# Holding six V blocks in SBUF, wider outer products and an earlier zero fill in a decode-step backward kernel

## The chip, the cores and the metric

The kernel runs on one core of a Trainium2 chip. The metric is the device time of one execution in microseconds (us), as the median of several executions. Every run quoted here is of the state that the records call fast. Ratios are the record's: fast runs of one kernel over fast runs of the other, so they are not quite the ratios of the medians that are quoted beside them.

The profile names the core's engines PE (matmuls; PEld loads their weights), DVE (vector operations), ACT (scalar operations), POOL (GpSimd) and SP (SyncE, which here only issues transfers). SBUF is the core's on-chip memory. Transfers run on 16 DMA engines.

## The reference

One decode step of a transformer layer with its backward pass: two batch rows, one query position, 32 query heads on 8 key/value heads, a cache of 32,768 positions of which the last W = 4,096 are attended, and a gated feed-forward network. It returns the output and the gradients of all inputs. Cut to what matters:

```python
W = min(4096, max(256, Sk // 4))
k = jnp.repeat(k_cache[:, :, Sk - W:, :], rep, axis=1)
v = jnp.repeat(v_cache[:, :, Sk - W:, :], rep, axis=1)
p = _softmax(jnp.einsum("bhqd,bhkd->bhqk", q, k) * Dh ** -0.5, axis=-1)
o = jnp.einsum("bhqk,bhkd->bhqd", p, v)
...
_out, _vjp = jax.vjp(_f, A_x, A_k_cache, A_v_cache, A_wq, A_wo, B_w_gate, B_w_up, B_w_down)
return (out, *_vjp(grad_out))
```

The gradients of the two caches have the caches' full shape, 2 x 8 x 32768 x 128 in bf16. Only the last 4,096 positions are not zero. So seven eighths of two 134 MB tensors must be written as zeros, 235 MB. That is the largest piece of work in the kernel.

## The kernel before

There are 16 blocks (2 batch rows x 8 key/value heads) of 4,096 x 128 values, 1 MB each. K and V are each read twice: once in the forward pass, and once in the backward pass, because they don't all fit in SBUF. Loads and results go through one queue (issued by SyncE, "the load queue"), the zeros through another (issued by GpSimd).

```python
# the zero fill: 32 jobs of 7 MB from one zero tile of 128 x 4096 (8 KB a partition)
zt = const.tile([P, Z], BF16, name="zero")
nc.vector.memset(zt[:], 0.0)
...
zf.dma_start(out=dst[:, a0:a1, :], in_=src)

# forward: oT = V^T P; a V block's buffer is free as soon as it has been used
for blk in range(NBLK):
    vb = b8.tile([P, KT, DH], BF16, tag="b8", name="vb")       # b8: 17 buffers of 8 KB a partition
    ld.dma_start(out=vb[:], in_=A_v_cache[b, g, R0:SK, :]...)
    for kt in range(KT):
        nc.tensor.matmul(out=oT_ps[...], lhsT=vb[:, kt, :], rhs=PTk[...], ...)
# ... output projection, feed-forward, its backward pass and weight gradients ...

# dV (and later dK): outer products, 32 rows x 128 columns at a time, 512 matmuls for each
def dkv_block(blk, S2, blk2, o_ap, nm):
    stg = b8.tile([P, KT, DH], BF16, tag="b8", name="stg_" + nm)
    for kt0 in range(0, KT, 2 * KG):
        for r in range(2):
            ...
            for i, kt in enumerate(kts):
                nc.tensor.matmul(out=ps[:, i, :], lhsT=S2[pb:pb + HQ, kt // 2, :], rhs=blk2[pb:pb + HQ, g, :], ...)
            evac(stg[:, kts[0]:kts[-1] + 1:2, :], ps[:, 0:n, :], "f32")
    ld.dma_start(out=o_ap[b, g, R0:SK, :]..., in_=stg[:])

# backward: all 16 V blocks are loaded again
for bank in range(NBANK):
    for bl in range(BPB):
        vb = b8.tile([P, KT, DH], BF16, tag="b8", name="vb2")
        ld.dma_start(out=vb[:], in_=A_v_cache[b, g, R0:SK, :]...)
        ...
```

## Time and profile before

| | before |
|---|---|
| median of 16 runs | 878.82 us (878.42 to 882.61) |
| span of the profiled run | 876.7 us |
| busy: PE, DVE, ACT | 48%, 32%, 23% |
| bytes moved | 364.13 MB, of which 234.88 MB zeros |
| mean rate | 415 GB/s |

From the page of the kernel before: the DMA rows of the table that cuts the span into 40 equal slices (busy tenths of the 16 DMA engines, and what they moved), then three lines of the queue table (packets, MB, share of the 16 engines' time). Queue q0 is the zero fill, q1 the load queue, q8 brings the PE's instructions.

```profile
DMA  8999999999999999999999999999999999999995
GB/s 343 426 425 425 426 426 426 426 427 425 426 426 426 425 423 420 417 414 418 419 419 419 404 425 425 426 425 426 423 425 422 419 423 420 428 420 422 420 421 214
...
q0 software_dynamic: 29184, 234.88, 64.0%
q1 hardware_dynamic: 18960, 128.47, 35.2%
q8 instruction: 42, 0.69, 0.3%
```

The transfer engines are full in 38 of 40 slices. No compute engine is at half. So a change gains only if it takes bytes away, raises the rate, or shortens the start or the tail.

The load queue's own waits of the kernel before, two lines of them (the waiting queue and line, what it waited for, us in total, times, longest):

```profile
SPq L560 <- DVE stg_dk L117: 151.1, 16, 24.8
SPq L688 <- DMA out_dram<-zero: 84.8, 1, 84.8
```

The first wait sits inside the chain of loads and results: a result waits for its eviction. It looks costly. The second says why it isn't: after its last result the load queue still waits 84.8 us for zeros. The chain may get longer by about that much before it sets the time.

The tail of the kernel before, in steps of 2 us (columns: window, its length, then busy us and instruction count of PE, PEld, DVE, ACT and POOL, the granted clock, the share of the DMA engines, GB/s):

```profile
862.00:864.00 2.00, 0.00 (x0) 0.00 (x0) 0.00 (x0) 0.00 (x0) 0.00 (x0) 0.50 0.89 373
864.00:866.00 2.00, 0.00 (x0) 0.00 (x0) 0.00 (x0) 0.00 (x0) 0.00 (x0) 0.50 0.44 184
866.00:868.00 2.00, 0.00 (x0) 0.00 (x0) 0.00 (x0) 0.00 (x0) 0.00 (x0) 0.50 0.26 111
868.00:870.00 2.00, 0.00 (x0) 0.00 (x0) 0.00 (x0) 0.00 (x0) 0.00 (x0) 0.50 0.16 70
870.00:872.00 2.00, 0.00 (x0) 0.00 (x0) 0.00 (x0) 0.00 (x0) 0.00 (x0) 0.50 0.13 53
872.00:874.00 2.00, 0.00 (x0) 0.00 (x0) 0.00 (x0) 0.00 (x0) 0.00 (x0) 0.50 0.06 25
```

Within 12 us the DMA share falls from 0.89 to 0.06: the 16 engines don't finish together. The last one alone holds the kernel open.

The issue of the first zero job in the kernel before (start, duration, engine, line, operation):

```profile
1.45 1.76 DVE L149 MEMSET zero<- 128x2048 uint32 x1 [0.38 <-issue]
...
3.53 1.00 POOL L185 DMA_DIRECT2D out_dram<-zero  x1 [1.72 <-DVE x_f L274]
```

And two lines of the costliest groups, the outer products (busy us, mean ns of one, idle time before them):

```profile
L557 PE MATMUL ps_dv<-DOblk,P_bf 32*128 32x128 bf16 x512 | 56.1, 295 | 0.2
...
L557 PE MATMUL ps_dk<-Qblk,dS_bf 32*128 32x128 bf16 x512 | 49.8, 299 | 8.3 <-DVE stg_dk L117 5.6
```

### The profile page before, as it was taken

The page shows a single profiled execution, that of the slowest core. Times are in us where ns is not written, and L with a number is a line of the kernel's source. Part 1 is how long each engine was busy: PE and PEld are TensorE (multiplying, and loading weights), DVE is VectorE, ACT ScalarE, POOL GpSimd, SP SyncE. Part 2 cuts the span into 40 slices and gives each one's busy share as a digit, 9 for nine tenths or more (in the row PEclk, how much of TensorE's full clock was granted, in tenths as well). Part 3 has the DMA queues.
Part 4 walks back from the last instruction along what each step waited for, and adds up shares of the span by engine and source line. Part 5 has one row for each costly group of instructions (what it writes and reads, how often), then busy time and mean ns, then how long its engine had stood idle before and what let it go on. Part 6 is the DMA issues. An engine that isn't in the chain of part 4 may idle for free.

```text
span 876.7 us, 12218 instructions
## 1 busy us (share of the span) xinstructions
PE 423.9 (48%) x5419; PEld 306.5 (35%) x5419; DVE 282.2 (32%) x428; ACT 197.4 (23%) x297; POOL 31.7 (4%) x49
## 2 busy tenths in 40 slices
PE   0777714236187664999400476784333332870000
PEld 0776604132154521376300466663222222420000
DVE  2233260011035679777300143353222221370000
ACT  0233320000023312666300132342211121240000
POOL 4000000000000000000000000000000000000000
PEclk9958755557579855555555587865555555865555
DMA  8999999999999999999999999999999999999995
GB/s 343 426 425 425 426 426 426 426 427 425 426 426 426 425 423 420 417 414 418 419 419 419 404 425 425 426 425 426 423 425 422 419 423 420 428 420 422 420 421 214
DMA packets 48197, 364.13 MB, mean 415 GB/s; under 512 B 2568, under 2 KB 2576, under 8 KB 4880
## 3 DMA queue, kind: packets, MB, share of 16 engines
q0 software_dynamic: 29184, 234.88, 64.0%
q1 hardware_dynamic: 18960, 128.47, 35.2%
q8 instruction: 42, 0.69, 0.3%
q14 instruction: 11, 0.09, 0.0%
HBM read 81.01 MB, written 282.33 MB: 414 GB/s over the span
## 4 chain that ended last, share of the span: by engine, by line
DMA 57%; PE 23%; DVE 6%; ACT 2%; issue 1%; SPq 1%; ACTq 0%; DVEq 0%
DMA kb<-in_A_k_cache_dram 26%; DMA vb<-in_A_v_cache_dram 21%; PE ps_dv L557 6%; DMA wd<-in_B_w_down_dram 5%; DMA out_dram<-stg_dv 5%; DVE dO_row L231 2%; PE tpb L242 2%; PE ps_wo L594 2%; PE ps_dk L557 2%; PE ps_wq L660 1%; PE dxn_ps L646 1%; PE dqT_ps L632 1%; PE tpw L643 1%; PE dxn_ps L506 1%; PE tpw L519 1%
## 5 line engine op out<-in xcount | busy, mean ns | idle before, releaser
L242 PE MATMUL tpb<-ident_bf,vb 128*128 128x128 bf16 x512 | 45.4, 266 | 82.3 <-DMA vb<-in_A_v_cache_dram 81.3
L117 DVE CAST stg_dk<-ps_dk 128x512 bf16<-128x512 f32 x64 | 42.4, 688 | 111.1 <-PE ps_dk L557 106.7
L242 PEld LDWEIGHTS <-vb 128*128 128x128 bf16 x512 | 41.8, 124 | 84.7 <-DMA vb<-in_A_v_cache_dram 82.9
L117 DVE COPY vt_sb<-tpb 128x1024 bf16<-128x1024 bf16 x39 | 26.4, 690 | 113.9 <-PE tpb L242 113.2
L115 ACT CAST stg_dk<-ps_dk 128x512 bf16<-128x512 f32 x64 | 36.6, 586 | 116.7 <-PE ps_dk L557 115.1
L632 PE MATMUL dqT_ps<-dSTk,kb 128*128 128x4 bf16 x512 | 16.3, 167 | 93.8 <-DMA kb<-in_A_k_cache_dram 93.8
L557 PE MATMUL ps_dv<-DOblk,P_bf 32*128 32x128 bf16 x512 | 56.1, 295 | 0.2
L242 PE MATMUL tpb<-ident_bf,kb 128*128 128x128 bf16 x512 | 48.2, 277 | 16.5 <-DMA kb<-in_A_k_cache_dram 16.1
L557 PE MATMUL ps_dk<-Qblk,dS_bf 32*128 32x128 bf16 x512 | 49.8, 299 | 8.3 <-DVE stg_dk L117 5.6
L185 POOL DMA_DIRECT2D out_dram<-zero x32 | 28.9, 986 | 678.4 <-DMA out_dram<-zero 676.7
L115 ACT COPY vt_sb<-tpb 128x1024 bf16<-128x1024 bf16 x25 | 25.1, 1013 | 122.0 <-PE tpb L242 110.5
L242 PEld LDWEIGHTS <-kb 128*128 128x128 bf16 x512 | 44.2, 129 | 18.5 <-DMA kb<-in_A_k_cache_dram 17.6
L632 PEld LDWEIGHTS <-kb 128*128 128x128 bf16 x512 | 15.0, 105 | 97.6 <-DMA kb<-in_A_k_cache_dram 97.2
L117 DVE CAST stg_dv<-ps_dv 128x512 bf16<-128x512 f32 x64 | 44.3, 691 | 12.0 <-PE ps_dv L557 9.5
L557 PEld LDWEIGHTS <-P_bf 32*128 32x128 bf16 x512 | 39.5, 122 | 17.4 <-issue 11.3
L117 DVE COPY kt_sb<-tpb 128x1024 bf16<-128x1024 bf16 x39 | 26.5, 690 | 57.2 <-PE tpb L242 52.3
L115 ACT CAST stg_dv<-ps_dv 128x512 bf16<-128x512 f32 x64 | 37.4, 585 | 18.9 <-PE ps_dv L557 18.9
L557 PEld LDWEIGHTS <-dS_bf 32*128 32x128 bf16 x512 | 31.5, 127 | 22.5 <-issue 21.2
L115 ACT COPY kt_sb<-tpb 128x1024 bf16<-128x1024 bf16 x25 | 25.2, 1012 | 54.4 <-PE tpb L242 45.5
L361 PE MATMUL oT_ps<-PTk,vb 128*128 128x4 bf16 x512 | 15.4, 167 | 42.0 <-DMA vb<-in_A_v_cache_dram 42.0
L361 PEld LDWEIGHTS <-vb 128*128 128x128 bf16 x512 | 14.6, 104 | 42.8 <-DMA vb<-in_A_v_cache_dram 42.8
L320 PE MATMUL st_ps<-QT_bf,kt_sb 128*128 128x4 bf16 x512 | 18.5, 166 | 4.7 <-ACT kt_sb L115 3.4
(203 smaller groups left out, 546.2 us busy)
## 6 DMA issues: line engine op xcount, KB each, us to landing
out_dram<-zero POOLq DMA_DIRECT2D x32, 7168.0 KB, 207.6
kb<-in_A_k_cache_dram SPq DMA_DIRECT2D x32, 1024.0 KB, 23.2
vb<-in_A_v_cache_dram SPq DMA_DIRECT2D x32, 1024.0 KB, 39.5
out_dram<-stg_dv SPq DMA_DIRECT2D x16, 1024.0 KB, 41.4
out_dram<-stg_dk SPq DMA_DIRECT2D x16, 1024.0 KB, 14.1
wq<-in_A_wq_dram SPq DMA_DIRECT2D x4, 1024.0 KB, 11.0
wo<-in_A_wo_dram SPq DMA_DIRECT2D x4, 1024.0 KB, 42.6
out_dram<-stg_wo SPq DMA_DIRECT2D x4, 1024.0 KB, 27.8
```

The source lines that it names most:

```text
L115: nc.scalar.copy(out=out, in_=in_)
L117: nc.vector.tensor_copy(out=out, in_=in_)
L185: zf.dma_start(out=dst[:, a0:a1, :], in_=src)
L231: nc.vector.tensor_copy(out=o, in_=ps[0:B, 0:n, :])
L242: nc.tensor.transpose(out=tp[:, i, :], in_=src[:, j0 + i, :], identity=ident_bf[:])
L320: nc.tensor.matmul(out=st_ps[:, bl, kt, :], lhsT=kt_sb[:, kt, :], rhs=QT_bf[:, b, g * REP:(g + 1) * REP], start=True, stop=True)
L361: nc.tensor.matmul(out=oT_ps[:, blk * REP:(blk + 1) * REP], lhsT=vb[:, kt, :], rhs=PTk[:, kt, blk * REP:(blk + 1) * REP], start=(kt == 0), ...
L506: nc.tensor.matmul(out=dxn2_ps[:], lhsT=dT_bf[:, r, :], rhs=wT[:].rearrange("p c d -> p (c d)"), start=(n_mm == 0), stop=(n_mm == 2 * FR - 1))
L519: nc.tensor.transpose(out=tp[:, c, :], in_=wo_slice(r)[:, c * P:(c + 1) * P], identity=ident_bf[:])
L557: nc.tensor.matmul(out=ps[:, i, :], lhsT=S2[pb:pb + HQ, kt // 2, :], rhs=blk2[pb:pb + HQ, g, :], start=True, stop=True, tile_position=(pb, 0))
L594: nc.tensor.matmul(out=ps[:], lhsT=o_row[:, r:HD:RW], rhs=dh_bf[:], start=True, stop=True)
L632: nc.tensor.matmul(out=dqT_ps[:, blk * REP:(blk + 1) * REP], lhsT=kb[:, kt, :], rhs=dSTk[:, kt, blk * REP:(blk + 1) * REP], start=(kt == 0 ...
```

## The change

Its intent is to take traffic out of a kernel bound by traffic, and to use the matmul array better. Six of the 16 V blocks stay in SBUF from the forward pass to the backward pass. The buffers for that come from smaller pools. The outer products take four 128-column tiles in one matmul of 128 rows x 512 columns, with a masked operand that puts zeros where heads don't belong together. The first two zero jobs are issued ahead of the masks. The core of the diff:

```diff
-    NB8=17,
+    NB8=19,
+    N_HOLD=6,
+    NWT=2,
...
-    b4 = ctx.enter_context(tc.tile_pool(name="b4", bufs=2))
-    t2k = ctx.enter_context(tc.tile_pool(name="t2k", bufs=4))
-    t4k = ctx.enter_context(tc.tile_pool(name="t4k", bufs=2))
-    tT = ctx.enter_context(tc.tile_pool(name="tT", bufs=2))
-    wt = ctx.enter_context(tc.tile_pool(name="wt", bufs=3))
+    b4 = ctx.enter_context(tc.tile_pool(name="b4", bufs=3))
+    t2k = ctx.enter_context(tc.tile_pool(name="t2k", bufs=3))
+    t4k = ctx.enter_context(tc.tile_pool(name="t4k", bufs=1))
+    tT = ctx.enter_context(tc.tile_pool(name="tT", bufs=1))
+    wt = ctx.enter_context(tc.tile_pool(name="wt", bufs=CFG["NWT"]))
...
-        nc.vector.memset(zt[:], 0.0)
+        nc.vector.memset(zt[:, 0:zh], 0.0)
+        ... nc.gpsimd.memset(zt[:, zh:Z], 0.0)
+    NZ_FIRST = 2
+    for o_, i_ in zjobs[:NZ_FIRST]:          # ahead of the identity and mask tiles
+        zf.dma_start(out=o_, in_=i_)
...
+        if blk >= NBLK - NHOLD:
+            v_held[blk] = vb
...
-    def dkv_block(blk, S2, blk2, o_ap, nm):
+    def dkv_block(blk, S4, X4t, o_ap, nm):
+        R = wt.tile([P, NS, DH], BF16, tag="wt", name="R_" + nm)
+        nc.vector.tensor_tensor(out=R[:], in0=_bcast(X4t[b][:], 1, NS), in1=_bcast(mask4[:, g, :], 2, DH), op=ALU.mult)
+        for kk in range(NQ):
+            nc.tensor.matmul(out=ps[:].rearrange("p s d -> p (s d)"), lhsT=S4[:, b, kk, :],
+                             rhs=R[:].rearrange("p s d -> p (s d)"), start=True, stop=True)
+            evac(stg[:, NS * kk:NS * kk + NS, :], ps[:], "f32")
...
+            if blk in v_held:
+                vb = v_held[blk]
+            else:
+                vb = b8.tile(...); ld.dma_start(...)
```

The probabilities are also kept in another layout for this (bf16, four tiles side by side). The rows of the attention output are built again where they are needed, which frees one 8 KB buffer early.

More of the change, by code (lines that the diff above doesn't have):

```diff
@@ L22 @@
     STOP=99,
-    RELIEF=(),
     HOLD_WQ=1,
+    ZORDER=0,
+    N_HOLD=6,
+    NWT=2,
 )
@@ L82 @@
     EPS = 1e-5
-    assert DH == P and NCOL * 2 == P and KT % 2 == 0 and D % P == 0 and F % P == 0 and D <= 512
+    assert DH == P and NCOL * 2 == P and KT % 4 == 0 and D % P == 0 and F % P == 0 and D <= 512
     assert HQ == 32 and W % P == 0
@@ L117, in evac @@
             nc.vector.tensor_copy(out=out, in_=in_)
+    x_bf = sm.tile([B, D], BF16, tag="sm", name="x_bf")
+    ld.dma_start(out=x_bf[:], in_=A_x[:, 0, :])
+    go_bf = keep.tile([B, D], BF16, name="go_bf")
+    ld.dma_start(out=go_bf[:], in_=grad_out[:, 0, :])
+    zjobs = []
+    if R0 > 0:
+        assert R0 % P == 0
+        per_part = (R0 // P) * DH
+        Z = _gdiv_le(per_part, CFG["ZMAX"])
+        na = per_part // Z
+        zt = const.tile([P, Z], BF16, name="zero")
+        zh = (Z // 2) if Z % 2 == 0 else Z
+        nc.vector.memset(zt[:, 0:zh], 0.0)
+        if zh < Z:
+            nc.scalar.activation(out=zt[:, zh:Z], in_=zt[:, 0:Z - zh], func=ACTF.Copy, scale=0.0) if False else nc.gpsimd.memset(zt[:, zh:Z], 0.0)
+        zap = zt[:]
+        nsplit = min(CFG["ZSPLIT"], na)
+        bounds = [(na * i) // nsplit for i in range(nsplit + 1)]
+        for t in (out_2, out_3):
+            for b in range(B):
+                for g in range(HKV):
+                    dst = t[b, g, 0:R0, :].rearrange("(p r) d -> p (r d)", p=P).rearrange("p (a z) -> p a z", z=Z)
+                    for i in range(nsplit):
+                        a0, a1 = bounds[i], bounds[i + 1]
+                        src = AP(zap.tensor, zap.offset, [list(zap.ap[0]), [0, a1 - a0], [1, Z]])
+                        zjobs.append((dst[:, a0:a1, :], src))
+    zo = CFG["ZORDER"]
+    if zo == 1:
+        h_ = len(zjobs) // 2
+        zjobs = zjobs[h_:] + zjobs[:h_]
+    elif zo == 2:
+        h_ = len(zjobs) // 2
+        zjobs = [j for pr in zip(zjobs[:h_], zjobs[h_:]) for j in pr]
+    elif zo == 3:
+        h_ = len(zjobs) // 2
+        zjobs = zjobs[:h_][::-1] + zjobs[h_:][::-1]
+    NZ_FIRST = 2
+    for o_, i_ in zjobs[:NZ_FIRST]:
+        zf.dma_start(out=o_, in_=i_)
     ident_bf = const.tile([P, P], BF16, name="ident_bf")
@@ L134 @@
                                 pattern=[[REP, HKV]], channel_multiplier=-1)
-    maskS = const.tile([P, HKV], F32, name="maskS")
-    nc.vector.tensor_scalar_mul(out=maskS[:], in0=mask1[:], scalar1=scale)
-    x_bf = sm.tile([B, D], BF16, tag="sm", name="x_bf")
-    ld.dma_start(out=x_bf[:], in_=A_x[:, 0, :])
-    go_bf = keep.tile([B, D], BF16, name="go_bf")
-    ld.dma_start(out=go_bf[:], in_=grad_out[:, 0, :])
-    if R0 > 0:
-        assert R0 % P == 0
-        per_part = (R0 // P) * DH
-        Z = _gdiv_le(per_part, CFG["ZMAX"])
-        na = per_part // Z
-        zt = const.tile([P, Z], BF16, name="zero")
-        nc.vector.memset(zt[:], 0.0)
-        zap = zt[:]
-        nsplit = min(CFG["ZSPLIT"], na)
-        bounds = [(na * i) // nsplit for i in range(nsplit + 1)]
-        relief = set(CFG["RELIEF"]) if (P == 128 and na * Z == per_part) else set()
-        PM = 120
-        rows_main = (PM * na * Z) // DH
-        NDUM = 17
-        rem_el = (R0 - rows_main - NDUM) * DH
-        ok_relief = (rows_main + NDUM < R0) and rem_el % 16 == 0
-        if ok_relief:
-            rem_row = rem_el // 16
-            rem_chunk = _gdiv_le(rem_row, Z)
-            ok_relief = rem_chunk >= 512
-        ridx = 0
-        for t in (out_2, out_3):
-            for b in range(B):
-                for g in range(HKV):
-                    if ok_relief and ridx in relief:
-                        pst = zap.ap[0][0]
-                        rows_q0 = R0 - rows_main
-                        d0 = t[b, g, 0:NDUM, :]
-                        src0 = AP(zap.tensor, zap.offset, [[pst, 1], [0, NDUM], [1, DH]])
-                        zf.dma_start(out=d0, in_=src0)
-                        zm = zt[P - PM:P, :]
-                        dstm = t[b, g, rows_q0:R0, :].rearrange("(p r) d -> p (r d)", p=PM).rearrange("p (a z) -> p a z", z=Z)
-                        srcm = AP(zm.tensor, zm.offset, [[pst, PM], [0, na], [1, Z]])
-                        zf.dma_start(out=dstm, in_=srcm)
-                        dstr = t[b, g, NDUM:rows_q0, :].rearrange("r d -> (r d)").rearrange("(p a z) -> p a z", p=16, z=rem_chunk)
-                        srcr = AP(zap.tensor, zap.offset, [[pst * 8, 16], [0, rem_row // rem_chunk], [1, rem_chunk]])
-                        zf.dma_start(out=dstr, in_=srcr)
-                    else:
-                        dst = t[b, g, 0:R0, :].rearrange("(p r) d -> p (r d)", p=P).rearrange("p (a z) -> p a z", z=Z)
-                        for i in range(nsplit):
-                            a0, a1 = bounds[i], bounds[i + 1]
-                            src = AP(zap.tensor, zap.offset, [list(zap.ap[0]), [0, a1 - a0], [1, Z]])
-                            zf.dma_start(out=dst[:, a0:a1, :], in_=src)
-                    ridx += 1
@@ L188, in layernorm_row @@
+    NS = 4
+    mask4 = const.tile([P, HKV, NS], F32, name="mask4")
+    nc.vector.memset(mask4[:], 0.0)
+    for s_ in range(NS):
+        nc.vector.tensor_copy(out=mask4[s_ * HQ:(s_ + 1) * HQ, :, s_], in_=mask1[s_ * HQ:(s_ + 1) * HQ, :])
+    for o_, i_ in zjobs[NZ_FIRST:]:
+        zf.dma_start(out=o_, in_=i_)
     def layernorm_row(src_f, name):
@@ L243, in transpose_block, with quad_transposes, q_cols @@
             evac(dst[:, j0:j0 + n, :], tp[:, 0:n, :], "bf")
-    def pair_transposes(srck, dst2):
+    NQ = KT // NS
+    def quad_transposes(srcq, dst4):
         G = 8
-        for k0 in range(0, KT // 2, G):
-            n = min(G, KT // 2 - k0)
-            tp = ps_tp.tile([P, G, P], BF16, tag="tp", name="tpp")
-            for i in range(n):
-                kk = k0 + i
-                nc.tensor.transpose(out=tp[:, i, :], in_=srck[:, 2 * kk:2 * kk + 2, :].rearrange("p a c -> p (a c)"),
-                                    identity=ident_bf[:])
-            evac(dst2[:, k0:k0 + n, :], tp[:, 0:n, :], "bf")
+        for b in range(B):
+            for k0 in range(0, NQ, G):
+                n = min(G, NQ - k0)
+                tp = ps_tp.tile([P, G, P], BF16, tag="tp", name="tpq")
+                for i in range(n):
+                    kk = k0 + i
+                    nc.tensor.transpose(out=tp[:, i, :], in_=srcq[:, kk, b, :, :].rearrange("p s m -> p (s m)"),
+                                        identity=ident_bf[:])
+                evac(dst4[:, b, k0:k0 + n, :], tp[:, 0:n, :], "bf")
+    def q_cols(tq, kt, blk):
+        b, g = divmod(blk, HKV)
+        return tq[:, kt // NS, b, kt % NS, g * REP:(g + 1) * REP]
     def ln_bwd(dxn_ps, xn, rstd, upstream_f, res):
@@ L266, in ln_bwd @@
         nc.vector.tensor_scalar_mul(out=s2[:], in0=s2[:], scalar1=-1.0 / D)
-        u = t2k.tile([B, D], F32, tag="t2k", name="lnb_u")
+        u = pr
         nc.vector.scalar_tensor_tensor(out=u[:], in0=xn[:], scalar=s2[:, 0:1], in1=t[:], op0=ALU.mult, op1=ALU.add)
@@ L298, with build_X4 @@
     nc.vector.tensor_copy(out=QT_bf[:], in_=QT_ps[:].rearrange("p h b -> p b h"))
-    QT_f2 = sm.tile([P, 2, B, HQ], F32, tag="sm", name="QT_f2")
-    nc.scalar.copy(out=QT_f2[:, 0, :, :], in_=QT_ps[:].rearrange("p h b -> p b h"))
-    nc.vector.tensor_copy(out=QT_f2[:, 1, :, :], in_=QT_f2[:, 0, :, :])
-    qh_ps = ps_acc.tile([P, P], F32, tag="acc", name="qh_ps")
-    nc.tensor.transpose(out=qh_ps[:], in_=QT_f2[:].rearrange("p r b h -> p (r b h)"), identity=ident_f[:])
-    Qblk2 = keep.tile([P, HKV, DH], BF16, name="Qblk2")
-    nc.vector.tensor_tensor(out=Qblk2[:], in0=_bcast(qh_ps[:], 1, HKV), in1=_bcast(maskS[:], 2, DH), op=ALU.mult)
+    QT_f = keep.tile([P, B, HQ], F32, name="QT_f")
+    nc.scalar.copy(out=QT_f[:], in_=QT_ps[:].rearrange("p h b -> p b h"))
+    def build_X4(XT_f, mul, nm):
+        tiles = []
+        for b in range(B):
+            rep = sm.tile([P, NS, HQ], F32, tag="sm", name=nm + "_rep")
+            nc.vector.tensor_copy(out=rep[:], in_=_bcast(XT_f[:, b, :], 1, NS))
+            hp_ = ps_acc.tile([P, P], F32, tag="acc", name=nm + "_hps")
+            nc.tensor.transpose(out=hp_[:], in_=rep[:].rearrange("p s h -> p (s h)"), identity=ident_f[:])
+            x4 = keep.tile([P, DH], BF16, name=f"{nm}_x4_{b}")
+            nc.scalar.activation(out=x4[:], in_=hp_[:], func=ACTF.Copy, scale=float(mul))
+            tiles.append(x4)
+        return tiles
     if CFG['STOP'] <= 1:
@@ L347 @@
     P_f = ST_sb
-    PTk = b4.tile([P, KT, NCOL], BF16, tag="b4", name="PTk")
-    nc.scalar.copy(out=PTk[:].rearrange("p k (b h) -> p b k h", h=REP), in_=P_f[:])
-    P_bf2 = b4.tile([P, KT // 2, P], BF16, tag="b4", name="P_bf2")
-    pair_transposes(PTk, P_bf2)
+    PTq = b4.tile([P, NQ, B, NS, HQ], BF16, tag="b4", name="PTq")
+    for b in range(B):
+        nc.scalar.copy(out=PTq[:, :, b, :, :].rearrange("p kk s (g h) -> p g kk s h", h=REP),
+                       in_=P_f[:, b * HKV:(b + 1) * HKV, :, :].rearrange("p g (kk s) h -> p g kk s h", s=NS))
+    P_bf4 = b4.tile([P, B, NQ, P], BF16, tag="b4", name="P_bf4")
+    quad_transposes(PTq, P_bf4)
     if CFG['STOP'] <= 2:
@@ L355 @@
     oT_ps = ps_acc.tile([P, NCOL], F32, tag="acc", name="oT_ps")
+    NHOLD = min(CFG["N_HOLD"], NBLK)
+    v_held = {}
     for blk in range(NBLK):
@@ L359 @@
         ld.dma_start(out=vb[:], in_=A_v_cache[b, g, R0:SK, :].rearrange("(p kt) d -> p kt d", p=P))
+        if blk >= NBLK - NHOLD:
+            v_held[blk] = vb
         for kt in range(KT):
             nc.tensor.matmul(out=oT_ps[:, blk * REP:(blk + 1) * REP], lhsT=vb[:, kt, :],
-                             rhs=PTk[:, kt, blk * REP:(blk + 1) * REP], start=(kt == 0), stop=(kt == KT - 1))
+                             rhs=q_cols(PTq, kt, blk), start=(kt == 0), stop=(kt == KT - 1))
     oT_f = keep.tile([P, NCOL], F32, name="oT_f")
@@ L369 @@
     otr_ps = row2col_ps(o_row, RW, RW, "otr", BF16)
-    OTr = sm.tile([P, RW, B], BF16, tag="sm", name="OTr")
+    OTr = keep.tile([P, RW, B], BF16, name="OTr")
     nc.vector.tensor_copy(out=OTr[:], in_=otr_ps[:])
@@ L530 @@
     nc.vector.tensor_copy(out=dOT_bf[:], in_=dot_ps[:].rearrange("p h b -> p b h"))
-    dOT_f2 = sm.tile([P, 2, B, HQ], F32, tag="sm", name="dOT_f2")
-    nc.scalar.copy(out=dOT_f2[:, 0, :, :], in_=dot_ps[:].rearrange("p h b -> p b h"))
-    nc.vector.tensor_copy(out=dOT_f2[:, 1, :, :], in_=dOT_f2[:, 0, :, :])
-    doh_ps = ps_acc.tile([P, P], F32, tag="acc", name="doh_ps")
-    nc.tensor.transpose(out=doh_ps[:], in_=dOT_f2[:].rearrange("p r b h -> p (r b h)"), identity=ident_f[:])
-    DOblk2 = keep.tile([P, HKV, DH], BF16, name="DOblk2")
-    nc.vector.tensor_tensor(out=DOblk2[:], in0=_bcast(doh_ps[:], 1, HKV), in1=_bcast(mask1[:], 2, DH), op=ALU.mult)
+    dOT_f = keep.tile([P, B, HQ], F32, name="dOT_f")
+    nc.scalar.copy(out=dOT_f[:], in_=dot_ps[:].rearrange("p h b -> p b h"))
+    XDO = build_X4(dOT_f, 1.0, "xdo")
     prod = sm.tile([P, NCOL], F32, tag="sm", name="prod")
-    nc.vector.tensor_tensor(out=prod[:], in0=oT_f[:], in1=dOT_f2[:, 0, :, :].rearrange("p b h -> p (b h)"), op=ALU.mult)
+    nc.vector.tensor_tensor(out=prod[:], in0=oT_f[:], in1=dOT_f[:].rearrange("p b h -> p (b h)"), op=ALU.mult)
     dl_ps = ps_acc.tile([P, NCOL], F32, tag="acc", name="dl_ps")
@@ L543 @@
     nc.vector.tensor_copy(out=delta_bc[:], in_=dl_ps[:].rearrange("p (b h) -> p b h", h=REP))
-    KG = 4
-    def dkv_block(blk, S2, blk2, o_ap, nm):
+    def dkv_block(blk, S4, X4t, o_ap, nm):
         b, g = divmod(blk, HKV)
+        R = wt.tile([P, NS, DH], BF16, tag="wt", name="R_" + nm)
+        nc.vector.tensor_tensor(out=R[:], in0=_bcast(X4t[b][:], 1, NS), in1=_bcast(mask4[:, g, :], 2, DH), op=ALU.mult)
         stg = b8.tile([P, KT, DH], BF16, tag="b8", name="stg_" + nm)
-        for kt0 in range(0, KT, 2 * KG):
-            for r in range(2):
-                kts = list(range(kt0 + r, min(KT, kt0 + 2 * KG), 2))
-                n = len(kts)
-                ps = ps_big.tile([P, KG, DH], F32, tag="big", name="ps_" + nm)
-                pb = r * NCOL + b * HQ
-                for i, kt in enumerate(kts):
-                    nc.tensor.matmul(out=ps[:, i, :], lhsT=S2[pb:pb + HQ, kt // 2, :], rhs=blk2[pb:pb + HQ, g, :],
-                                     start=True, stop=True, tile_position=(pb, 0))
-                evac(stg[:, kts[0]:kts[-1] + 1:2, :], ps[:, 0:n, :], "f32")
+        for kk in range(NQ):
+            ps = ps_big.tile([P, NS, DH], F32, tag="big", name="ps_" + nm)
+            nc.tensor.matmul(out=ps[:].rearrange("p s d -> p (s d)"), lhsT=S4[:, b, kk, :],
+                             rhs=R[:].rearrange("p s d -> p (s d)"), start=True, stop=True)
+            evac(stg[:, NS * kk:NS * kk + NS, :], ps[:], "f32")
         ld.dma_start(out=o_ap[b, g, R0:SK, :].rearrange("(p kt) d -> p kt d", p=P), in_=stg[:])
@@ L589 @@
         n = min(HP, RW - r0)
+        o_r = t4k.tile([B, HP, P], BF16, tag="t4k", name="o_r")
+        col2row(OTr[:, r0:r0 + n, :], n, o_r[:, 0:n, :].rearrange("b j p -> b (j p)"))
         stg = b8.tile([P, HP, D], BF16, tag="b8", name="stg_wo")
         for j in range(n):
-            r = r0 + j
             ps = ps_big.tile([P, D], F32, tag="big", name="ps_wo")
-            nc.tensor.matmul(out=ps[:], lhsT=o_row[:, r:HD:RW], rhs=dh_bf[:], start=True, stop=True)
+            nc.tensor.matmul(out=ps[:], lhsT=o_r[:, j, :], rhs=dh_bf[:], start=True, stop=True)
             evac(stg[:, j, :], ps[:], "f32")
@@ L598 @@
     for blk in range(NBLK):
-        dkv_block(blk, P_bf2, DOblk2, out_3, "dv")
+        dkv_block(blk, P_bf4, XDO, out_3, "dv")
     if CFG['STOP'] <= 6:
         return
-    dSTk = b4.tile([P, KT, NCOL], BF16, tag="b4", name="dSTk")
-    for bank in range(NBANK):
+    dSTq = b4.tile([P, NQ, B, NS, HQ], BF16, tag="b4", name="dSTq")
+    bank_order = sorted(range(NBANK), key=lambda bk: -sum(1 for bl in range(BPB) if (bk * BPB + bl) in v_held))
+    for bank in bank_order:
         dp_ps = ps_big.tile([P, BPB, KT, REP], F32, tag="big", name="dp_ps")
-        for bl in range(BPB):
+        bl_order = sorted(range(BPB), key=lambda bl: 0 if (bank * BPB + bl) in v_held else 1)
+        for bl in bl_order:
             blk = bank * BPB + bl
             b, g = divmod(blk, HKV)
-            vb = b8.tile([P, KT, DH], BF16, tag="b8", name="vb2")
-            ld.dma_start(out=vb[:], in_=A_v_cache[b, g, R0:SK, :].rearrange("(p kt) d -> p kt d", p=P))
+            if blk in v_held:
+                vb = v_held[blk]
+            else:
+                vb = b8.tile([P, KT, DH], BF16, tag="b8", name="vb2")
+                ld.dma_start(out=vb[:], in_=A_v_cache[b, g, R0:SK, :].rearrange("(p kt) d -> p kt d", p=P))
             vt_sb = b8.tile([P, KT, P], BF16, tag="b8", name="vt_sb")
@@ L618 @@
         nc.vector.tensor_tensor(out=T[:], in0=dp_ps[:], in1=_bcast(delta_bc[:, bs, :], 2, KT), op=ALU.subtract)
-        nc.vector.tensor_tensor(out=dSTk[:, :, bank * BPB * REP:(bank + 1) * BPB * REP].rearrange("p k (b h) -> p b k h", h=REP),
-                                in0=T[:], in1=P_f[:, bs, :, :], op=ALU.mult)
-    dS_bf2 = b4.tile([P, KT // 2, P], BF16, tag="b4", name="dS_bf2")
-    pair_transposes(dSTk, dS_bf2)
+        for b in range(B):
+            lo = max(bank * BPB, b * HKV)
+            hi = min((bank + 1) * BPB, (b + 1) * HKV)
+            if lo >= hi:
+                continue
+            g0, g1 = lo - b * HKV, hi - b * HKV
+            for s_ in range(NS):
+                o_v = dSTq[:, :, b, s_, g0 * REP:g1 * REP].rearrange("p kk (g h) -> p g kk h", h=REP)
+                nc.vector.tensor_tensor(out=o_v, in0=T[:, lo - bank * BPB:hi - bank * BPB, s_:KT:NS, :],
+                                        in1=PTq[:, :, b, s_, g0 * REP:g1 * REP].rearrange("p kk (g h) -> p g kk h", h=REP), op=ALU.mult)
+    dS_bf4 = b4.tile([P, B, NQ, P], BF16, tag="b4", name="dS_bf4")
+    quad_transposes(dSTq, dS_bf4)
+    XQ = build_X4(QT_f, scale, "xq")
     if CFG['STOP'] <= 7:
@@ L632 @@
             nc.tensor.matmul(out=dqT_ps[:, blk * REP:(blk + 1) * REP], lhsT=kb[:, kt, :],
-                             rhs=dSTk[:, kt, blk * REP:(blk + 1) * REP], start=(kt == 0), stop=(kt == KT - 1))
-        dkv_block(blk, dS_bf2, Qblk2, out_2, "dk")
+                             rhs=q_cols(dSTq, kt, blk), start=(kt == 0), stop=(kt == KT - 1))
+        dkv_block(blk, dS_bf4, XQ, out_2, "dk")
     dQT2_bf = sm.tile([P, HQ, B], BF16, tag="sm", name="dQT2_bf")
```

## The prediction

> **What bounds the kernel now.** Transfers. In the table of 40 slices the 16 DMA engines are busy in tenths 9 in 38 slices, moving 404 to 428 GB/s there; all compute engines are below half (PE 48%, DVE 32%, ACT 23%). The queue table has 364.13 MB: 234.88 MB of zero fill, 128.47 MB of loads and results. The waits of the load queue end with 84.8 us for the zero fill: from about 790 us only zeros move. The chain of waits names K and V loads (26% and 21%), but shortening that chain alone buys nothing: while the load queue stalls (260 to 340 us) the zero fill takes the whole 421 to 425 GB/s. So the time is bytes / rate, plus start and tail. The Trainium skill ("DMA: Bandwidth & Descriptors", Issuing engines are not separate DMA queues) says that DMAs from any engine share the same 16 engines and interleave; this trace agrees (425 GB/s in total with both queues or one).
>
> Not at full rate: the start (343 GB/s in the first slice, about 4 us lost) and the tail, where the rate falls from 422 at 862 us to 184, 111, 70, 53, 25 GB/s in steps of 2 us, because the DMA engines finish unevenly: about 10 us lost.
>
> **What the change does.** (a) Six of 16 V blocks stay in SBUF and aren't loaded again: 6 x 1.049 = 6.29 MB less. At 424 GB/s that is 14.8 us, and since the DMA engines are full all the time, nearly all of it should show. (b) dK/dV outer products: 512 matmuls of 32 rows x 128 columns (295 ns each) become 128 of 128 x 512 (this width took 525 to 600 ns elsewhere: an estimate of 67 to 77 us against 56), plus 16 mask products per pass on DVE (about 0.7 us each, as a 128x512 eviction). Off the critical path. (c) About 1,470 fewer PE instructions in the program; the instruction queue moved 0.69 MB in 42 packets, so some 6 packets fewer: perhaps 1 us of the tail. (d) The zero fill is issued before the masks. The first issue stood at 3.53 us behind a 1.76 us memset; now half of it runs on POOL, which took 0.2 us for 128x128: an estimated 1.8 us. Gain 0 to 0.5 us, since weight loads already fill the engines from 2 us on. (e) Held V crowds the buffers: in the built program both w_down tiles have one slot, so the second load waits for the first's use (an estimated 20 us more in the load chain, from the 47 us load and 14 transposes). The zero fill uses that time; the load queue has 85 us in hand.
>
> **Sum.** 879.1 - 14.8 - 1 (tail) - 0.3 (start) = 863.0 us, range 859.5 to 867. Ratio 0.982, close to the 2% line (861.5): faster by over 2% 0.25, within 2% 0.72, slower 0.03.
>
> **Right if** the queue table shows about 122.2 MB on the load queue and 234.88 MB of zeros; the mean rate stays 414 to 417 GB/s; the last wait of the load queue is still for zeros (60 to 110 us); HBM reads fall from 81.0 to about 74.7 MB.
>
> **Wrong if** the load chain ends after the zeros (results still landing in the last slices, below 400 GB/s): buffer pressure would then set the time, above 870 us. Or if the tail is not from uneven instruction traffic: a tail 5 us longer or shorter moves the time as much, and a gain over 2.5 us beyond the bytes makes it faster by over 2%.

## The result

The changed kernel took 862.83 us (median of 8 runs, 862.28 to 865.06), the kernel before 878.82 us. The ratio of the fast runs is 0.9818, with a 95% interval of 0.9807 to 0.983. The predicted ratio was 0.982.

The page of the changed kernel, the same lines:

```profile
DMA  8999999999999999999999999999999999999995
GB/s 339 426 426 423 426 427 426 427 426 426 427 426 426 427 424 422 418 415 418 418 416 417 406 419 427 424 427 426 423 422 419 422 422 421 425 422 420 418 421 245
...
q0 software_dynamic: 29184, 234.88, 65.3%
q1 hardware_dynamic: 18096, 122.18, 34.2%
q8 instruction: 36, 0.59, 0.2%
```

The load queue has 122.18 MB (predicted 122.2), the zeros 234.88 MB. The engines are as full as before. HBM reads fell from 81.01 to 74.72 MB (predicted 74.7), and the mean rate is 416 GB/s (predicted 414 to 417). The PE's instructions came in 36 packets instead of 42.

Two of the load queue's waits in the changed kernel:

```profile
SPq L713 <- DMA out_dram<-zero: 87.2, 1, 87.2
...
SPq L437 <- DMA wd<-in_B_w_down_dram: 37.9, 1, 37.9
```

The queue still ends with a wait for zeros, 87.2 us (predicted 60 to 110): the load chain is still not what counts. The other line is new. Both w_down tiles share a buffer, so the second load waits. In the chain of waits it lands at 261.8 us, against 245.9 us for the w_down loads of the kernel before: 16 us of delay in the chain (an estimated 20 was predicted), and nothing to see of it in the time. The wait comes with the held blocks: without them (hold0, below) both loads are issued by 208.1 us, as in the kernel before.

The tail of the changed kernel, columns as above:

```profile
846.00:848.00 2.00, 0.00 (x0) 0.00 (x0) 0.00 (x0) 0.00 (x0) 0.00 (x0) 0.50 0.93 393
848.00:850.00 2.00, 0.00 (x0) 0.00 (x0) 0.00 (x0) 0.00 (x0) 0.00 (x0) 0.50 0.79 332
850.00:852.00 2.00, 0.00 (x0) 0.00 (x0) 0.00 (x0) 0.00 (x0) 0.00 (x0) 0.50 0.35 147
852.00:854.00 2.00, 0.00 (x0) 0.00 (x0) 0.00 (x0) 0.00 (x0) 0.00 (x0) 0.50 0.27 115
854.00:856.00 2.00, 0.00 (x0) 0.00 (x0) 0.00 (x0) 0.00 (x0) 0.00 (x0) 0.50 0.12 49
856.00:858.00 2.00, 0.00 (x0) 0.00 (x0) 0.00 (x0) 0.00 (x0) 0.00 (x0) 0.50 0.14 57
```

It is a little shorter. The next section puts numbers to that.

The first zero job in the changed kernel:

```profile
0.80 1.80 POOL L136 MEMSET zero<- 128x2048 bf16 x1 [0.29 <-POOLq L702]
...
3.77 1.00 POOL L160 DMA_DIRECT2D out_dram<-zero  x1
```

It is issued later than before (3.77 us, not 3.53), although the change issues it ahead of the masks. The zero half on POOL takes 1.8 us. The source has the issue next, but in the trace POOL first starts two memsets and one select of the identity tiles (2.54 to 3.82 us); why they come first isn't shown. The first slice of the page has 339 GB/s (before: 343). The predicted 0.3 us of gain at the start did not come.

The outer products of the changed kernel:

```profile
L567 PE MATMUL ps_dk<-R_dk,dS_bf 128*128 128x512 bf16 x127 | 53.8, 550 | 3.1 <-ACT stg_dk L117 1.5
...
L567 PE MATMUL ps_dv<-R_dv,P_bf 128*128 128x512 bf16 x128 | 40.1, 394 | 15.9 <-ACT stg_dv L117 11.0
```

dV fell from 56.1 to 40.1 us of PE, and dK rose from 49.8 to 53.8 us.

### Two numbers instead of one: when the DMA engines finish

Every zero job ends with 16 small writes of 4 bytes (512 in the records, for 32 jobs), one by each DMA engine, when that engine's part has landed. For the last zero job of a profiled run, the 16 times say when each engine was done. Their mean is the time that the bytes need. What the last engine adds to the mean is called its lag here. These times are read from the trace's records of single transfers, since no view of the profile lists them. They are of one execution each, the profiled one. In hold0, hold0b and hold3 (below) the last engine is so late that its write for the job before falls among the last 16; that write is left out here. The expectations still have the figures with it in (865.3 us, lags of 17.5 and 15.1 us).

```
kernel                     mean finish  last engine  lag   sorted: the last four, relative to the mean
before                        866.0        875.0      9.0   +2.8 +3.0 +5.8 +9.0
changed                       851.3        858.5      7.2   +2.4 +2.6 +7.0 +7.2
```

The mean moved by 14.7 us; six blocks of 1.049 MB at 424 GB/s are 14.8 us. The rest of the 16 us is the lag (1.8 us in this pair of profiles). In every profiled run but relief, hold0r and wide (below), the measured time is 3.7 to 3.8 us above the last engine's finish, so the time is the mean finish, plus the lag, plus that.

### The profile page after: what moved, and what is told of

The parts are those of the page before. It is cut to its first block, busy times and chain, and to the rows that moved or that the text cites. A ratio compares the mean times of both kernels' runs of the same rounds, so it can differ in the third digit from the quotient of the medians.

```text
span 860.2 us, 10760 instructions
## 1 busy us (share of the span) xinstructions
PE 419.7 (49%) x4684; PEld 261.5 (30%) x4685; DVE 301.3 (35%) x480; ACT 198.0 (23%) x302; POOL 33.7 (4%) x50
## 2 busy tenths in 40 slices
DMA packets 47326, 357.73 MB, mean 416 GB/s; under 512 B 2472, under 2 KB 2480, under 8 KB 4784
## 3 DMA queue, kind: packets, MB, share of 16 engines
q0 software_dynamic: 29184, 234.88, 65.3%
q1 hardware_dynamic: 18096, 122.18, 34.2%
HBM read 74.72 MB, written 282.33 MB: 415 GB/s over the span
## 4 chain that ended last, share of the span: by engine, by line
DMA 51%; PE 24%; DVE 8%; ACT 4%; issue 2%; SPq 1%; ACTq 0%; DVEq 0%
DMA kb<-in_A_k_cache_dram 23%; DMA vb<-in_A_v_cache_dram 17%; DMA wd<-in_B_w_down_dram 6%; DMA out_dram<-stg_dv 4%; PE tpb L241 3%; PE ps_dk L567 3%; PE ps_dv L567 2%; DVE dO_row L230 2%; ACT stg_dv L117 2%; PE ps_wo L605 2%; PE ps_wq L685 1%; PE tpw L668 1%; PE dxn_ps L671 1%; PE c2r_ps L227 1%; PE tpw L522 1%
## 5 line engine op out<-in xcount | busy, mean ns | idle before, releaser
L241 PE MATMUL tpb<-ident_bf,vb 128*128 128x128 bf16 x512 | 51.7, 274 | 35.6 <-DMA vb<-in_A_v_cache_dram 26.0
L241 PE MATMUL tpb<-ident_bf,kb 128*128 128x128 bf16 x512 | 46.3, 271 | 39.5 <-DMA kb<-in_A_k_cache_dram 39.1
L657 PE MATMUL dqT_ps<-dSTq,kb 128*128 128x4 bf16 x512 | 16.0, 166 | 98.3 <-DMA kb<-in_A_k_cache_dram 98.3
L567 PE MATMUL ps_dk<-R_dk,dS_bf 128*128 128x512 bf16 x127 | 53.8, 550 | 3.1 <-ACT stg_dk L117 1.5
L185 POOL DMA_DIRECT2D out_dram<-zero x30 | 26.9, 930 | 661.3 <-DMA out_dram<-zero 661.3
L657 PEld LDWEIGHTS <-kb 128*128 128x128 bf16 x512 | 14.8, 103 | 109.7 <-DMA kb<-in_A_k_cache_dram 108.8
L567 PE MATMUL ps_dv<-R_dv,P_bf 128*128 128x512 bf16 x128 | 40.1, 394 | 15.9 <-ACT stg_dv L117 11.0
L380 PE MATMUL oT_ps<-PTq,vb 128*128 128x4 bf16 x512 | 15.6, 167 | 42.8 <-DMA vb<-in_A_v_cache_dram 42.8
L380 PEld LDWEIGHTS <-vb 128*128 128x128 bf16 x512 | 14.7, 104 | 43.6 <-DMA vb<-in_A_v_cache_dram 43.6
L567 PEld LDWEIGHTS <-P_bf 128*128 128x128 bf16 x128 | 12.1, 98 | 43.4 <-issue 31.3
L567 PEld LDWEIGHTS <-dS_bf 128*128 128x128 bf16 x128 | 14.0, 118 | 29.0 <-issue 27.6
L630 PE MATMUL dp_ps<-dOT_bf,vt_sb 128*128 128x4 bf16 x512 | 19.4, 167 | 3.7 <-ACT vt_sb L117 2.0
## 6 DMA issues: line engine op xcount, KB each, us to landing
out_dram<-stg_dk SPq DMA_DIRECT2D x16, 1024.0 KB, 13.8
```

The costliest lines, as they stand in the source:

```text
L185: zf.dma_start(out=o_, in_=i_)
L241: nc.tensor.transpose(out=tp[:, i, :], in_=src[:, j0 + i, :], identity=ident_bf[:])
L380: nc.tensor.matmul(out=oT_ps[:, blk * REP:(blk + 1) * REP], lhsT=vb[:, kt, :], rhs=q_cols(PTq, kt, blk), start=(kt == 0), stop=(kt == KT - 1))
L567: nc.tensor.matmul(out=ps[:].rearrange("p s d -> p (s d)"), lhsT=S4[:, b, kk, :], rhs=R[:].rearrange("p s d -> p (s d)"), start=True, stop ...
L630: nc.tensor.matmul(out=dp_ps[:, bl, kt, :], lhsT=vt_sb[:, kt, :], rhs=dOT_bf[:, b, g * REP:(g + 1) * REP], start=True, stop=True)
L657: nc.tensor.matmul(out=dqT_ps[:, blk * REP:(blk + 1) * REP], lhsT=kb[:, kt, :], rhs=q_cols(dSTq, kt, blk), start=(kt == 0), stop=(kt == KT ...
```

## Experiments

Theories. *Bytes*: while zeros are the last to land, the time is bytes over rate, plus start and lag; each held block is worth 2.47 us, and whatever happens in the load chain is free as long as the chain ends before the zeros. *Chain*: the time follows the chain of waits through the K and V loads, and the gain comes from the outer products or the order of the loads. For the lag: *instruction traffic* on single DMA engines, against any other cause. Twelve kernels ran (two of them repeats), all with correct results, in three groups of four. The kernels of a group ran on the same chip and shared the runs of the kernel before, whose medians there were 879.21, 879.07 and 878.87 us.

### 1. No block held (hold0, and once more as hold0b)

```diff
-    N_HOLD=6,
+    N_HOLD=0,
```

> The changed kernel with no V block held, all else of the change kept: 6.29 MB more to load. Bytes theory (every held block is worth 1.049 MB / 424 GB/s = 2.47 us): 862.8 + 14.8 = 877.6 us, load queue back at 128.5 MB, and about 1 us under the kernel before, for its shorter tail (36 instruction packets instead of 42). Rival (the saved PE work and the changed order of the zero fill make the gain, the bytes hide behind the zero fill): about 863 us, within 3 us.

> The kernel with no block held again: two groups of times were seen, 877.4 and 885.5 us. If only the last engine's lag differs between executions, the mean finish stays 865.3 us (within 0.5 us) in whatever group the profiled run falls; in the fast group the lag is near 9 us, in the slow one near 17 us. If the rate differed, the mean would move with the time.

Measured: 884.94 us median in the first group and 885.65 us in the second. The times fall in two groups: 877.3, 877.5 and 877.5 us, and 884.9 to 886.6 us in eight runs, with one at 881.2. (The kernel before has late runs too: 7 of its 49 took 882.6 to 884.7 us, the others at most 881.3.) The ratio to the kernel before was 1.002 (0.9979 to 1.0061), then 1.0039 (1.0004 to 1.0075). The page of hold0:

```profile
GB/s 345 426 424 425 424 429 425 427 426 424 427 425 426 425 426 420 415 417 418 419 418 406 422 425 424 426 425 427 426 422 422 423 423 426 426 422 418 421 418 51
...
q1 hardware_dynamic: 18960, 128.47, 34.9%
q8 instruction: 36, 0.59, 0.2%
```

The quick runs are where the bytes theory put them (877.6 us). The others are 8 us above, and at first sight that contradicts it. The last slice (51 GB/s) says where to look. The tail of hold0:

```profile
868.00:872.00 4.00, 0.00 (x0) 0.00 (x0) 0.00 (x0) 0.00 (x0) 0.00 (x0) 0.50 0.09 37
872.00:876.00 4.00, 0.00 (x0) 0.00 (x0) 0.00 (x0) 0.00 (x0) 0.00 (x0) 0.50 0.06 27
876.00:880.00 4.00, 0.00 (x0) 0.00 (x0) 0.00 (x0) 0.00 (x0) 0.00 (x0) 0.50 0.06 27
```

From 872 us on there is a share of 0.06 and 27 GB/s: one of 16 engines is still at work, alone, for ten microseconds. In both profiles the mean finish is where the bytes put it, and the lag is twice as long:

```
hold0                         865.0        882.8     17.8   -0.4 +3.3 +4.3 +17.8
hold0b                        865.2        882.4     17.2   +1.2 +2.8 +4.2 +17.2
```

So holding six blocks moves the mean from about 865.1 to 851.3 us, 13.8 us, and the lag decides what of it the clock shows: by medians the six blocks are worth 22 us (884.94 to 862.83), of which about 14 us are the bytes and the rest is a shorter lag. Both profiles fell in the slow group, so that the quick group has the short lag is inferred from its times and not seen. The chain theory (about 863 us without held blocks) is refuted by both groups.

### 2. Three blocks held (hold3), and three blocks held in the old kernel (bh3)

```diff
# hold3, on the changed kernel
-    N_HOLD=6,
+    N_HOLD=3,
# bh3, on the kernel before: old outer products, old zero fill, three blocks held,
# the backward pass takes the blocks in reverse order
-    NB8=17,
+    NB8=19,
+    N_HOLD=3,
...
+        if blk >= NBLK - CFG["N_HOLD"]:
+            v_held[blk] = vb
...
+            if blk in v_held:
+                vb = v_held[blk]
+            else:
```

In bh3 the buffers are paid for with the same small pools as in the change. (The cut leaves out the pools and the reversed loops.)

> Three V blocks held instead of six. Bytes theory: linear in the bytes, halfway between none and six, 870.2 us (within 1 us). Rival: the first held blocks already bring all of it, or none of it, because the load chain is what counts: 863 or 877 us.

> The kernel before with one thing of the change alone: three V blocks held (two more buffers, paid for by the spare ones of the small pools), old outer products, old order of the zero fill. Bytes theory: the DMA engines finish 3 x 2.47 = 7.4 us earlier on average, about 871.5 us, and the load queue moves 125.3 MB. Rival (the new outer products make the gain): 879 us. A second term is known by now: the engine that finishes last was 9.0 us behind the mean in the profiled run before, 7.2 in the changed kernel, 17.5 and 15.1 with none and three blocks held there. If the lag grows here too, the time lies above 871.5 by as much, and the mean of the engines must still be 7.4 us earlier.

Measured: hold3 876.12 us (873.46 to 876.91), ratio 0.9947 (0.9917 to 0.9978), 6 us above what was expected. bh3 872.13 us (871.92 to 872.45), ratio 0.9916 (0.9895 to 0.9937), within 0.7 us of it.

```
hold3                         857.8        873.1     15.3   +2.2 +3.6 +15.3
bh3                           858.9        868.7      9.8   +4.6 +6.7 +9.8
```

Both means sit where three blocks put them: near halfway between 865.1 and 851.3 us for hold3 (858.2), and 7.1 us under 866.0 us for bh3 (expected 7.4). From the page of bh3 (the kernel before had 128.47 MB here):

```profile
q1 hardware_dynamic: 18528, 125.32, 34.6%
```

bh3 is the cleanest test, because one part of the change alone (with the pools and the block order that it needs), in the old kernel, brings its full worth of bytes. hold3 missed by its lag, one late engine as in hold0.

### 3. A longer load chain (slack)

```diff
+    for _ in range(160):
+        nc.tensor.matmul(out=dmy_ps[:], lhsT=xn2_bf[:, 0:P], rhs=go_bf[:], start=True, stop=True)
```

These stand between the dV pass and the second V pass.

> The changed kernel with 160 useless wide matmuls (about 0.55 us each, 88 us) between the dV pass and the second V pass, where PE waits some 35 us anyhow: the load chain gets about 50 us later, with 320 instructions and no bytes more. Bytes theory: the time stays at 863 us (within 1.5 us), and the last wait for the zero fill shrinks from 87 us to about 35 us. Rival (the chain of waits through K and V loads sets the time): about 910 us.

Measured: 865.07 us (862.38 to 866.04), ratio 0.9822: 2 us above the expected 863, outside its 1.5 us, and 45 us under the rival's 910. A piece of the chain of waits (start, us, what), and the last wait of the load queue:

```profile
457.00 65.46 PE dmy_ps L618 x160
```

```profile
SPq L718 <- DMA out_dram<-zero: 63.2, 1, 63.2
```

The dummies took 65 us, not 88 (410 ns each), and they stand in the chain that ended last with all 65 us. The last wait shrank from 87.2 to 63.2 us: the chain got 24 us longer, less than the 50 that were intended. The mean finish is 851.3 us, the same as without them, and the lag is 9.7 us. So 24 us more in the chain cost nothing that could be told from the lag. The chain theory wanted that much more time. A view that puts nearly half of the span down to K and V loads (25.7% and 21.1% in the kernel before) says nothing of what shortening them would bring.

### 4. More instructions (dummy)

```diff
+    for _ in range(512):     # once before the second V pass, once at the end
+        nc.tensor.matmul(out=dmy_ps[:], lhsT=go_bf[:, 0:2], rhs=go_bf[:, 0:2], start=True, stop=True)
```

> The changed kernel with 1,024 tiny useless matmuls (2,048 PE instructions, 8 instruction packets of 16 KB more), half before the second V pass, half at the end where PE is idle. If instruction fetches fall mostly on the DMA engine that finishes last, at 0.93 us a packet: up to 7 us more, about 869 us, with a longer tail. If they spread evenly over the engines, or the tail has another cause: under 0.5 us more, 863 us. The prediction's 1 us for 6 packets would be about 1.3 us here, 864 us.

Measured: 866.4 us (866.24 to 866.55), ratio 0.9842; that is 3.6 us over the changed kernel's 862.83. The instruction queue's line:

```profile
q8 instruction: 44, 0.72, 0.3%
```

There are eight packets more than in the changed kernel (44, not 36), of 0.72 MB / 44 = 16 KB each.

```
dummy                         851.3        862.5     11.2   +2.4 +2.6 +11.0 +11.2
```

The mean stayed at 851.3 us. Two engines were late in the changed kernel, by 7.0 and 7.2 us, and two are late here, by 11.0 and 11.2 us. Two engines that share 8 packets of 0.93 us (their mean duration in the records) would be 3.7 us later each, so the fit is good. It is no proof. The excess depends on what one compares with: it is 3.6 us over the changed kernel's first runs, 2.7 us over its repeat (after2, 863.74 us), and 1.3 us over slack, which ran on the same chip. And lags of 9.1 us (after2) and 10.2 us (more7b) came with 36 packets.

The records don't name the engines, but where only zeros move the engines can be told apart, since nearly every packet starts 3 or 4 ns before the previous packet of its engine ends. Followed in this way from 285 to 315 us of the changed kernel, three instruction packets fall on three different engines. Each of these needed 18.4 to 18.5 us for its part of that zero job, where most others needed 17.1 us, so a packet held its engine for about 1.3 us. None of the three was the engine that finished these jobs last, 4.8 to 6.0 us after the mean. That one carried no instruction packet there; its own zero packets were longer, 312 to 319 ns on average in the jobs that could be followed, where 309 ns was the usual. hold0's two packets between 290 and 320 us are not on its last engine either.

So in the stretch that can be followed, instruction traffic is not what makes the last engine late. Where loads run beside the zeros, the packets could not be followed with certainty. What made dummy's two engines 4 us later than in the changed kernel, why one engine's packets are longer, and why hold0 has one late engine and the changed kernel two, stays open. The prediction's "1 us for 6 packets" is not confirmed.

### 5. Work taken from the last engine (relief, hold0r)

```diff
+    # the last zero job in three pieces: all 128 partitions for 4 (hold0r: 2) of 7 columns,
+    # then 120 partitions, then 8, for the rest
+    zf.dma_start(out=o_l[:, 0:AR, :], in_=AP(zap.tensor, zap.offset, [[pst_, P], [0, AR], [1, Z]]))
+    zf.dma_start(out=o_l[0:120, AR:na, :], in_=AP(zap.tensor, zap.offset, [[pst_, 120], [0, na - AR], [1, Z]]))
+    zf.dma_start(out=o_l[120:128, AR:na, :], in_=AP(zap.tensor, zap.offset, [[pst_, 8], [0, na - AR], [1, Z]]))
```

relief is on the changed kernel, hold0r on the one without held blocks. The split was meant to take work from one of the 16 engines, here called the last; that a piece of 120 partitions leaves one engine out was assumed, and no run shows it.

> The changed kernel with the last zero job split: four sevenths as before on all 16 DMA engines[...]. If the late engine is always the last one: it finishes with the others and the time falls by 1 to 5 us. If late engines are others (two of them were 7 us late in the changed kernel): no gain, 863 to 864 us, and one engine 7 us early in the records of the last transfers.

> The changed kernel with no block held (877.3 to 886.6 us, mostly 885) and the same split of the last zero job[...]. If its one late engine (17.5 us behind the mean) is the last engine: about 873 us in its usual runs, and no more two groups of times. If it is another: 886 us or more.

Measured: relief 869.03 us (868.36 to 872.58), ratio 0.989; hold0r 894.25 us (889.46 to 898.34), ratio 1.0171. Both are slower than their kernels without the split. (hold0r's "886 us or more" is met by the number, but not for its reason.) Windows of relief, first one with the usual zero jobs, then one in the split job:

```profile
800.00:830.00 30.00, 0.00 (x0) 0.00 (x0) 0.00 (x0) 0.00 (x0) 0.00 (x0) 0.50 1.01 419
842.00:850.00 8.00, 0.00 (x0) 0.00 (x0) 0.00 (x0) 0.00 (x0) 0.00 (x0) 0.50 0.92 244
```

The engines are nearly as busy (0.92), but they move 244 GB/s instead of 419. In the records 116 of the 238 packets of 8 KB in this window took over 550 ns, where 309 is usual. So the split pieces are themselves slow (which of the two, the records don't say), and the runs say nothing of which engine is late. That is a failed experiment for its question.

### 6. A seventh block (more7, more7b), and wider packets (wide)

```diff
# more7 and more7b: t4k tiles moved to b8, tT tiles to t2k, and
-    NB8=19,  N_HOLD=6,
+    NB8=20,  N_HOLD=7,
# more7 alone                      # more7b alone
-    ZMAX=4096,                    -    b4 ... bufs=3
+    ZMAX=2048,                    +    b4 ... bufs=2
# wide
-    NB8=19,  N_HOLD=6,  ZMAX=4096,
+    NB8=18,  N_HOLD=5,  ZMAX=7168,
```

> The changed kernel with a seventh V block held, in a 20th buffer, paid for by a zero tile of half the width (4 KB packets instead of 8 KB in the zero fill) and by two small pools merged into others. Bytes theory: 1.049 MB less, 860.4 us, unless the smaller packets of the zero fill cost rate: then the rate of the slices in which only zeros move falls below 420 GB/s, and 1% of it costs 5.5 us.

> A seventh V block held, now with the full zero tile and its 8 KB packets; the 20th buffer is paid for by three small pools (two probability buffers instead of three, two pools merged into others). Bytes theory: 1.049 MB less, mean finish 2.5 us earlier than in the changed kernel (848.8 us), time 860.4 us if the last engine's lag stays near 7 us. If buffer pressure counts: over 863 us, with the last wait for zeros below 60 us.

> The changed kernel with zero packets of 14 KB instead of 8 KB (a wider zero tile), paid for by one buffer and one held block fewer (1.049 MB more). If each packet has a fixed cost (4 KB packets fell to 401 GB/s where only zeros moved, 8 KB made 419): where only zeros move the rate rises to about 430 GB/s, and the time falls to about 860 us in spite of the 2.5 us for the block. If 8 KB packets are already at the limit: 865.3 us.

Measured: more7 880.37 us (880.13 to 880.68), ratio 1.001; more7b 862.57 us (860.04 to 862.93), ratio 0.9798 (0.9773 to 0.9824); wide 906.37 us (905.02 to 907.46), ratio 1.0302. more7 missed its 860.4 us because its rate fell, as its expectation allowed; wide was expected at 860 or 865.3 us and missed both by over 40 us. By the author's account a build with an eighth block in 20 buffers deadlocked in the simulator and was not run.

A window in which only zeros move, first of the changed kernel (8 KB packets), then of more7 (4 KB packets), and the last wait of more7's load queue:

```profile
800.00:840.00 40.00, 0.00 (x0) 0.00 (x0) 0.00 (x0) 0.00 (x0) 0.00 (x0) 0.50 1.01 419
```

```profile
800.00:840.00 40.00, 0.00 (x0) 0.00 (x0) 0.00 (x0) 0.00 (x0) 0.00 (x0) 0.50 1.02 401
```

```profile
SPq L711 <- DMA out_dram<-zero: 260.4, 1, 260.4
```

4 KB packets move 401 GB/s where 8 KB packets move 419. And they changed the sharing: from 60 to 160 us the two queues moved equal numbers of packets in every kernel, if the 4-byte completion writes are counted too (changed 2,769 of zeros and 2,767 of loads, more7 3,768 and 3,768, wide 2,014 and 2,016). The zeros' part of the rate is therefore set by their packet size: 223 GB/s with 8 KB, 153 with 4 KB, 280 with 14 KB. In more7 the zeros fell behind, the loads were done early (last wait 260.4 us instead of 87.2), and the zeros went on alone at the lower rate.

wide is the counterpart. The DMA rows of its page:

```profile
DMA  8999999999999999999999999999999999979704
GB/s 342 432 425 426 428 428 429 428 427 430 429 430 428 428 430 430 430 426 431 428 423 423 424 426 423 422 421 422 410 417 425 422 424 424 380 260 357 292 1 186
```

The rate is higher (425 to 432 GB/s in the first 20 slices but the first), but the zeros took so much of it that they were done by 790 us. The load chain, starved until then, was left with only its own transfers and waits: in the last slices the engines idle (DMA tenths 9, 7, 0, 4) and the kernel ends at 904 us. Here the load chain sets the time. This is the case that the prediction named as its way to be wrong, brought about by accident: neither branch of wide's expectation had it. The question that wide was built for has an answer in its trace: where only zeros and four instruction packets move, in the same stage of the work, 14 KB packets made 429 GB/s (364 to 430 us), 8 KB packets 424 (changed kernel, 272 to 338 us) and 4 KB packets 408 (more7, 208 to 274 us).

more7b keeps the 8 KB packets, and its mean finish is 848.9 us, 2.4 us under 851.3 us, as the bytes say; its lag was 10.2 us in the profile. Its best run (860.04 us) is the best of the study. Against the changed kernel on the same chip (after2, below: 863.74 us) its median is 1.2 us lower; the lag hides the rest of the 2.5 us.

### 7. The changed kernel again (after2)

> The changed kernel again, unaltered, as a control on the chip of the next three: 862 to 865 us, the engines finishing at 851.3 us on average as in its first profile (within 0.5 us, since the bytes fix it), the last one 5 to 10 us after that.

Measured: 863.74 us (862.02 to 866.09), ratio 0.9817. Mean finish 850.9 us, lag 9.1 us (7.2 in its first profile). So the lag moves by 2 us between executions of one program, and the mean by 0.4.

## Why the prediction was right

- *What bounds the kernel*: right. Mean finish against megabytes moved: 866.0 us for 364.13, 865.0 for 364.02, 858.9 for 360.97, 857.8 for 360.88, 851.3 for 357.73, 848.9 for 356.68. From the first to the last that is 17.1 us for 7.45 MB, or 436 GB/s; this includes whatever the rest of the change brings to the mean (hold0 is 1.0 us under the kernel before).
- *(a) 14.8 us for six blocks*: right, 14.7 us in the mean finish for the whole change. The blocks alone bring 13.8 us of it (from hold0 and hold0b to the changed kernel), and bh3 shows the same worth per block in the old kernel (7.1 us for three).
- *(b) outer products*: right that they are off the critical path. The size was off: 67 to 77 us of PE for each pass was estimated, 40.1 us (dV, 394 ns each) and 53.8 us (dK, 550 ns each) were measured. The term had been sized with matmuls of the same width elsewhere (526 ns at a granted clock of 0.71, 598 ns at 0.50); dV ran at 0.71 from 380 to 420 us and at 1.00 from 420 to 458 us, dK at 0.57 to 0.67 from 560 to 690 us.
- *(c) 1 us of the tail*: the pair of profiles gives 1.8 us, but the reason given, fewer instruction packets, isn't confirmed. hold0 has the changed kernel's 36 packets and a lag of 17.8 us, against 9.0 us with 42 packets in the kernel before. The lag is 7 to 18 us over the kernels and moves by 2 us between executions. With the long lag of hold0 the same bytes would have ended over 10 us higher (17.8 against 7.2), the risk that the prediction named last. That the total came out within 0.2 us is partly luck.
- *(d) 0.3 us at the start*: wrong in sign. The first zero job was issued 0.24 us later; the estimated 1.8 us for POOL's half of the zero tile was exact, but POOL's identity setup, which the trace has ahead of the issue, was overlooked.
- *(e) the load chain has room*: right. 16 us more from w_down and another 24 us from the dummies did not move the mean finish, and wide shows what happens when the room is gone.

## What to carry to other kernels

When the DMA engines are full from start to end, count bytes: each one removed is worth its share of the rate, and a longer chain of waits costs nothing as long as another queue has work to fill the gaps and still ends last. Check that last condition by the final wait of the queue, since the packet size of one queue also sets how much of the rate the other gets. Below a per cent, look at when each DMA engine finishes: the last one, not the mean, ends the kernel. What makes it late is not settled here.

## What the Trainium skill lacked or had wrong

- "DMA: Bandwidth & Descriptors", Issuing engines are not separate DMA queues: that all DMAs share 16 engines and interleave agrees with these runs. The page gives no figures for the shares that follow: two queues moved equal counts of packets whatever their sizes (2,769 and 2,767 in 100 us of the changed kernel), so 14, 8 and 4 KB zero packets got 280, 223 and 153 GB/s beside loads in pieces of mostly 8 KB (experiment 6).
- "DMA: Bandwidth & Descriptors", Why a DMA increments its semaphore by 16 and not by 1: the section tells how many engines a shape gets, but not that the shape can cost rate. A zero job split into pieces of 120 and 8 partitions moved 244 GB/s in an 8 us window, and the usual one from 128 moved 419 GB/s (experiment 5). Why isn't shown by these runs.
- "Runtime: NRT & Kernel Launch", Instruction fetch mechanics: that instructions come in 16 KiB blocks agrees (0.72 MB in 44 packets). What it lacks is the cost on a full DMA engine: one that carried a block needed 18.4 us for its part of a zero job instead of 17.1 us (experiment 4).
- "HBM Reference", Specifications (TRN2): that a core alone can stream at about 425 GB/s agrees (423 to 427 GB/s in the changed kernel's slices 2 to 15). Zeros alone moved 419 GB/s from 800 to 840 us, and 401 GB/s in 4 KB packets.
- "DMA: Bandwidth & Descriptors", Latency and other measured facts: it says that two of the 16 engines, 7 and 15, are usually slower, with an uncertain cause. Two engines were late together in the changed kernel (7.0 and 7.2 us), but one in hold0 (17.8 us), and these records don't name engines. What it lacks is the size of the effect at the end of a long kernel (7 to 18 us between the mean and the last engine), and that one program's times can fall in two groups 8 us apart.
